# Zero products ahead of the first matmuls, another order of the first K chunks, a bf16 exp, and FFN norms two steps later, in four interleaved layers

## The chip, the core and the metric

The kernel runs on one NeuronCore of a Trainium2 chip. A core has a matrix engine (TensorE, "PE" in the profile; its weight loads are shown as "PEld"), three engines for elementwise work (VectorE, "DVE"; ScalarE, "ACT"; GpSimd, "POOL"), and SyncE ("SP"), whose queue here issues all the transfers. Each engine works through its own list of instructions in order and waits on semaphores for what others make. Data lie in SBUF (128 partitions), products in PSUM (eight banks of 128 x 512 fp32). The metric is the device time of one execution in microseconds; 0.2% of it is about 3 us.

## The reference

Four layers over x of shape (1, 2048, 1024) in bf16: A, B, A, B, each with a residual and a normalization ahead of it. A is linear attention with 32 heads of width 32, B is a gated feed-forward block (FFN) with F = 3584.

```python
def A(x, wqkv, wo):
    q, k, v = split(x @ wqkv)                       # 32 heads of 32
    phi = lambda t: where(t > 0, t + 1, exp(t)) + 1e-6
    pq, pk = phi(q), phi(k)
    kv = einsum("bhsd,bhse->bhde", pk, v)
    z = einsum("bhsd->bhd", pk)
    num = einsum("bhqd,bhde->bhqe", pq, kv)
    den = einsum("bhqd,bhd->bhq", pq, z)[..., None] + 1e-6
    return (num / den).merge_heads() @ wo

def B(x, w_gate, w_up, w_down):
    return ((x @ w_gate) * (x @ w_up)) @ w_down

x = A_x
for _ in range(2):
    x = x + A(layernorm(x), A_wqkv, A_wo)
    x = x + B(layernorm(x), B_w_gate, B_w_up, B_w_down)
```

## The kernel before

X stays in SBUF for the whole program, as 16 tiles of 128 tokens; four tiles make a group of 512 tokens. The order of all work is written out by hand: what the program records first on an engine runs first there. Buffers come from three free lists, in the order in which they were put back: 16 slots of 128 x 4096 bf16, 13 temporaries of 128 x 512 fp32, eight PSUM banks.

**Start (L99 to L143, L918 to L925).** SP issues the loads of X tiles 0 and 1, the first 512 columns of K's weights (a "slab" of 1 MB, L96), X tiles 2 and 3, the second K slab, X 4, the first V slab, and so on. Then, for tiles 0 to 3, the normalization is recorded: `ln_stats` (DVE: two `bn_stats` L158, one aggregation L159), `ln_norm` (ACT: the reciprocal deviation as a Ln L166 and an Exp L168; DVE: L170 writes the normalized tile `xn`). Only tile 0 is also transposed there. `tr_tile` transposes a normalized tile: for the first group of the first layer by eight PE products with the identity (L187) and one ACT copy (L188), in all other places by a transposing DMA on SP's queue (L182).

**Layer A (`layer_A`, L359).** First 64 chunks of eight matmuls (`kv_chunk`, L369): for each group of 512 tokens the eight K chunks (four tiles, two slabs), then the eight V chunks. A K chunk goes through `phi`: ACT takes the exp of the bank into a temporary (L193), DVE takes min with 1 and adds 1e-6 in place (L194), and adds max(x, 0) from the bank (L195). A V chunk is copied by ACT (L377). At given chunk numbers a plan calls other work: statistics, norms and transposes of the tiles of the next group, the product of K features and V (`kp`, L386), and, in the first layer, scans of the FFN weights for their norms (ACT squares L202, DVE statistics L207). In the first layer the transposes of tiles 1, 2 and 3 stand behind chunks 0, 1 and 3, so PE's order is: transposes of tile 0, chunk of tile 0 with slab 0, transposes of tile 1, chunk of tile 0 with slab 1, transposes of tile 2, chunk of tile 1 with slab 0, and so on.

Then comes a loop over steps i = 0 to 43 (L528). Step i takes the denominators of feature block i - 4 (`den_step`: PE L501, ACT L503 and L506, DVE L509), the Q product of block i (`q_step`: eight matmuls L487, then `phi`), and the output product i - 12 (`out_step`: eight matmuls L517, DVE adds to X at L519). An output product of a group needs all eight feature blocks of that group, so the one of step 20 waits for the L509 of step 19. In the first layer, rows of the down weights are scanned in between (ACT L220, DVE L222). At the end of each step what `ahead_of` (L894) has planned for the FFN is called: for tile u = 0 to 7 its statistics at step 18 + 2u, its norm one step later and its transpose DMA two steps later; weight loads, casts (ACT L312) and sums (DVE L327); and sums over the transposed X (`t_sums`, DVE L349 to L357) at steps 36 to 39. In the first layer the loads and GpSimd casts of raw down weights (L566, L571) start at steps 36 and 40.

**Layer B (`layer_B`)** computes the FFN with seven block products instead of eight, on PE at L646 (gate and up) and L868 (down); its lines are not touched.

Of the kernel before, what the change touches and what calls it, by code (L numbers as in the profile page):

```python
# [9 lines left out]
ACT = mybir.ActivationFunctionType  # L10
ALU = mybir.AluOpType
AX = mybir.AxisListType
BF16 = mybir.dt.bfloat16
F16 = mybir.dt.float16
F32 = mybir.dt.float32
# [19 lines left out]
def kernel(  # L35
# [11 lines left out]
    nc = tc.nc  # L47
    P = 128
# [3 lines left out]
    KD = D // P  # L52
    KH = KD // 2
    KF = F // P
    G = 512
    NG = S // G
    TPG = G // P
    NB = 512
    DC = D // NB
# [7 lines left out]
    small = ctx.enter_context(tc.tile_pool(name="small", bufs=4))  # L67
# [6 lines left out]
    wqkv_v = A_wqkv.rearrange("(k p) n -> p k n", p=P)  # L74
# [7 lines left out]
    temps = Free([const.tile([P, NB], F32, tag=f"f{i}", name=f"f{i}") for i in range(13)])  # L82
    banks = Free([psum.tile([P, NB], F32, tag=f"b{i}", name=f"b{i}") for i in range(8)])

    def v3(s, n):
        return s[:].rearrange("p (k n) -> p k n", n=n)
# [4 lines left out]
    def load_x(t):  # L91
        nc.sync.dma_start(out=X[:, t, :], in_=x_view[:, t, :])

    def load_cols(view, n):
        s = slots.get()
        nc.sync.dma_start(out=v3(s, NB), in_=view[:, :, n * NB:(n + 1) * NB])  # L96
        return s

    nc.scalar.preload_act_table_set("natural_log_exp_and_others")  # L99
    wA = {}  # L100
    load_x(0)
    load_x(1)
    wA["k"] = [load_cols(wqkv_v, DC)]
    load_x(2)
    load_x(3)
    wA["k"].append(load_cols(wqkv_v, DC + 1))
    load_x(4)
    wA["v"] = [load_cols(wqkv_v, 2 * DC)]
    load_x(5)
    load_x(6)  # L110
    wA["v"].append(load_cols(wqkv_v, 2 * DC + 1))
    for t in range(7, NT):
        load_x(t)

    ident = const.tile([P, P], BF16, tag="ident", name="ident")
    make_identity(nc, ident[:])
    mask = const.tile([P, P], F32, tag="mask", name="mask")
# [30 lines left out]
    NST = D // FMAX  # L148
# [2 lines left out]
    xqs = {}  # L151
    lns = {}

    def ln_stats(li, t):
        mv = small.tile([P, 2], F32, tag="mv", name="mv")
        st = small.tile([P, NST, 6], F32, tag="st", name="st")
        for c in range(NST):
            nc.vector.bn_stats(out=st[:, c, :], in_=X[:, t, c * FMAX:(c + 1) * FMAX])  # L158
        nc.vector.bn_aggr(out=mv[:], in_=st[:])  # L159
        lns[(li, t)] = mv  # L160

    def ln_norm(li, t):
        mv = lns[(li, t)]
        half = li % 2 == 1
        rstd = small.tile([P, 1], F32, tag="rstd", name="rstd")
        nc.scalar.activation(out=rstd[:], in_=mv[:, 1:2], func=ACT.Ln, bias=(eps5x if half else eps5)[:],  # L166
                             scale=1.0 / (XS * XS) if half else 1.0)
        nc.scalar.activation(out=rstd[:], in_=rstd[:], func=ACT.Exp, scale=-0.5)  # L168
        xn = xnp.tile([P, D], F16 if half else BF16, tag="xn", name="xn")
        nc.vector.tensor_scalar(out=xn[:], in0=X[:, t, :], scalar1=mv[:, 0:1], scalar2=rstd[:],  # L170
                                op0=ALU.subtract, op1=ALU.mult)
        lns[(li, t)] = xn

    def tr_tile(li, t):
        xn = lns.pop((li, t))
        g, tl = divmod(t, TPG)
        if (li, g) not in xnTs:
            xnTs[(li, g)] = slots.get()
        s = xnTs[(li, g)]
        xnT = (h3 if li % 2 == 1 else v3)(s, NB)  # L180
        if (li, g) != (0, 0):
            nc.sync.dma_start_transpose(out=xnT[:, :, tl * P:(tl + 1) * P], in_=xn[:])  # L182
            return
        b = banks.get()
        pt = b[:].bitcast(BF16).rearrange("p (k n) -> p k n", n=P)
        for k in range(KD):
            nc.tensor.transpose(out=pt[:, k, :], in_=xn[:, k * P:(k + 1) * P], identity=ident[:])  # L187
        nc.scalar.copy(out=xnT[:, :, tl * P:(tl + 1) * P], in_=pt)  # L188
        banks.put(b)

    def phi(b, dst):
        m = temps.get()
        nc.scalar.activation(out=m[:], in_=b[:], func=ACT.Exp)  # L193
        nc.vector.tensor_scalar(out=m[:], in0=m[:], scalar1=1.0, scalar2=1e-6, op0=ALU.min, op1=ALU.add)  # L194
        nc.vector.scalar_tensor_tensor(out=dst, in0=b[:], scalar=0.0, in1=m[:], op0=ALU.max, op1=ALU.add)  # L195
        temps.put(m)

    def scan(i):
# [160 lines left out]
    def layer_A(li, ahead):  # L359
# [3 lines left out]
        def kv_chunk(t, n):  # L363
            g, tl = divmod(t, TPG)
            xnT = v3(xnTs[(li, g)], NB)
            w = v3(wA["k"][n] if n < DC else wA["v"][n - DC], NB)
            b = banks.get()
            for k in range(KD):
                nc.tensor.matmul(out=b[:], lhsT=xnT[:, k, tl * P:(tl + 1) * P], rhs=w[:, k, :],  # L369
                                 start=(k == 0), stop=(k == KD - 1))  # L370
            if n < DC:
                if g not in pks:
                    pks[g] = slots.get()
                phi(b, v3(pks[g], D)[:, tl, n * NB:(n + 1) * NB])
            else:
                c0 = (n - DC) * (NB // P)
                nc.scalar.copy(out=vbs[t % NV][:, c0:c0 + NB // P, 0:P],  # L377
                               in_=b[:].rearrange("p (c f) -> p c f", f=P))
            banks.put(b)
# [15 lines left out]
        def at(step, f, *args):  # L395
            plan.setdefault(step, []).append((f, args))

        NCH = 2 * DC * TPG
        for t in range(TPG, NT):
            i = (t // TPG - 1) * NCH + 3 * (t % TPG)  # L400
            at(i + 3, ln_stats, li, t)
            at(i + 5, ln_norm, li, t)
            at(i + 6, tr_tile, li, t)
        for t in range(NT - TPG):
            at((t // TPG + 1) * NCH + 3, kp, t)
        if li == 0:
            for t, i in ((1, 0), (2, 1), (3, 3)):
                at(i, tr_tile, li, t)
        at(2 * NCH + 4, lambda: wA.update(q=[load_cols(wqkv_v, n) for n in range(DC)]))
        at(3 * NCH + 4, lambda: wA.update(o=[load_cols(wo_v, n) for n in range(DC)]))  # L410
        if li == 0:
# [12 lines left out]
            for i, t0, t1 in ((10, 16, 24), (0, 16, 25), (1, 16, 28), (2, 20, 31), (3, 32, 36), (11, 32, 39),  # L424
# [3 lines left out]
                at(t1, spend, i, 0)  # L428
                at(t1 + 1, spend, i, 1)
        for i in range(NG * NCH):  # L430
            q, j = divmod(i, NCH)
            half, j = divmod(j, DC * TPG)
            tl, n = divmod(j, DC)
            kv_chunk(q * TPG + tl, half * DC + n)
            for f, args in plan.get(i, []):
                f(*args)
        slots.put(*wA.pop("k"), *wA.pop("v"))
# [43 lines left out]
        def q_step(g, c):  # L481
            xnT = v3(xnTs[(li, g)], NB)
            w = v3(wA["q"][c // (NB // P)], NB)
            j = c % (NB // P)
            b = banks.get()
            for k in range(KD):
                nc.tensor.matmul(out=b[:], lhsT=w[:, k, j * P:(j + 1) * P], rhs=xnT[:, k, :],  # L487
                                 start=(k == 0), stop=(k == KD - 1))
            pq[(g, c)] = temps.get()
            phi(b, pq[(g, c)][:].bitcast(BF16)[:, 0:G])  # L490
            banks.put(b)
            if c == KD - 1:
                slots.put(xnTs.pop((li, g)))
                if g == NG - 1:
                    slots.put(*wA.pop("q"))
# [279 lines left out]
    def down_seven(q, li, p, hs, wd, load_piece, cast_piece, ORDER, at, run, finish, xrow, nl, W2, load_a, final):  # L775
# [31 lines left out]
        if nl[0] < 4:  # L807
            for u in range(2 * TPG if p == 0 else TPG):
                t = nl[1] * 2 * TPG + u
                at(2 + 7 * u, ln_stats, nl[0], t)  # L810
                at(4 + 7 * u, ln_norm, nl[0], t)
                at(5 + 7 * u, tr_tile, nl[0], t)
# [81 lines left out]
    def ahead_of(li, W):  # L894
        plan = {}

        def at(step, *what):
            plan.setdefault(step, []).append(what)

        for u in range(2 * TPG):  # L900
            at(18 + 2 * u, ln_stats, li, u)
            at(19 + 2 * u, ln_norm, li, u)
            at(20 + 2 * u, tr_tile, li, u)
        at(22, W.load, 0)
        at(28, W.load, 1)
        for i in range(4):
            at(25 + i, W.cast, 0, i)
            at(34 + i, W.cast, 1, i)
            at(36 + i, t_sums, li, 0, i)
        at(35, W.sums, 0)  # L910
        at(41, W.sums, 1)
        if li == 1:
            at(36, prep_load, 0)
            at(38, prep_load, 1)
            at(40, prep_cast, 0)
        return plan

    for t in range(TPG):  # L918
        ln_stats(0, t)
        ln_norm(0, t)  # L920
        if t == 0:
            tr_tile(0, 0)
    for li in (0, 2):
        W = Weights(li)
        layer_A(li, ahead_of(li + 1, W))  # L925
        layer_B(li + 1, W)
# [30 lines left out]
```

## Time and profile before

| | |
|---|---|
| Median of three runs | 1515.85 us (1515.51 to 1516.08) |
| The profiled execution, its own time | 1515.59 us |
| its span, first to last instruction | 1513.8 us |
| PE busy | 1499.7 us (99%), 7155 matmuls |
| DVE busy | 952.5 us (63%) |
| ACT busy | 736.2 us (49%) |
| POOL busy | 90.0 us (6%) |
| DMA engines, mean share | 51.6% on SP's queue, 164 GB/s |

The profile is one execution. The span leaves out what lies before the first and behind the last instruction, so it is 1.79 us shorter than the execution's own time. "Busy" counts overlapping matmuls once; a PE that is 99% busy can still run at a lower clock. A line such as `L369 PE MATMUL b<-s,s` names the line of the kernel, the engine, the operation, and the buffers written and read (`b` a bank, `s` a slot, `f` a temporary). Where an instruction's engine was idle before it, the idle time and what ended it stand in brackets.

The program's stretches, by PE's lines in the chain that ended last: opening until 20.5 us, K and V of the first layer until 130 us, its Q and output steps until 255.8 us, the first FFN until 763.5 us, then the second pair of layers.

### The profile page before, as it was taken

To read this page: it belongs to the slowest core of one execution; us is meant where nothing else is said; L and a number is where in the kernel's file an instruction comes from. 1 tells how busy PE (TensorE), PEld (TensorE's weight loads), DVE (VectorE), ACT (ScalarE), POOL (GpSimd) and SP (SyncE) were. 2 spreads that over 40 slices of the span, in tenths; PEclk is the share of its full clock that TensorE was granted. 3 is DMA by queue.
4 is the path that set the end of the run, shared out by engine and by line. 5 is a ranking of instruction groups with operands and counts; after the bars stand their busy time and mean duration, and the time that the engine had idled before them with its cause. 6 is when DMAs were issued, how large, how long until landed. Compare 5 with 4: busy or idle time off the path is not lost.

```text
span 1513.8 us, 18314 instructions
## 1 busy us (share of the span) xinstructions
PE 1499.7 (99%) x7155; PEld 689.1 (46%) x7155; DVE 952.5 (63%) x1595; ACT 736.2 (49%) x1111; POOL 90.0 (6%) x46
## 2 busy tenths in 40 slices
PE   7999999999999999999999999999999999999999
PEld 3454444444444444444445444444444444444444
DVE  6567998988677566667355467854444853444452
ACT  4677875777535477762133365523334222333420
POOL 0000004963000000000000000000000000000000
PEclk9999999999999999999999999999999999999999
DMA  7696246475358788758413300563333678333523
GB/s 239 152 302 225 84 90 189 121 218 159 117 135 240 239 264 263 243 197 247 160 28 84 84 1 8 148 234 139 140 111 129 165 258 342 113 139 139 193 75 129
DMA packets 213399, 247.61 MB, mean 164 GB/s; under 512 B 68416, under 2 KB 189248, under 8 KB 202560
## 3 DMA queue, kind: packets, MB, share of 16 engines
q1 hardware_dynamic: 213312, 246.44, 51.6%
q8 instruction: 56, 0.92, 0.2%
q14 instruction: 31, 0.25, 0.0%
HBM read 189.79 MB, written 40.89 MB: 152 GB/s over the span
## 4 chain that ended last, share of the span: by engine, by line
PE 94%; DVE 4%; ACT 1%; DMA 1%; issue 0%; SPq 0%
PE b L646 45%; PE b L868 22%; PE b L369 12%; PE b L517 6%; PE b L487 6%; PE b L386 1%; DVE dmx L222 1%; PE b L501 1%; ACT s L202 1%; DVE wst L207 1%; DVE f L195 1%; DMA s<-in_A_wqkv_dram 1%; DVE f L194 1%; ACT f L193 0%; DVE s L195 0%; PE b L469 0%
## 5 line engine op out<-in xcount | busy, mean ns | idle before, releaser
L646 PE MATMUL b<-s,s 128*128 128x512 f16 x3136 | 677.5, 379 | 0.0
L646 PEld LDWEIGHTS <-s 128*128 128x128 f16 x3136 | 306.9, 98 | 370.0
L868 PE MATMUL b<-s,s 128*128 128x512 f16 x1568 | 339.1, 379 | 0.0
L662 DVE TENSOR_TENSOR f<-f,b 128x512 f32<-128x512 f32 x232 | 159.0, 686 | 229.1 <-ACT f L651 214.6
L651 ACT COPY f<-b 128x512 f32<-128x512 f32 x284 | 165.9, 584 | 228.0 <-PE b L646 228.0
L868 PEld LDWEIGHTS <-s 128*128 128x128 f16 x1568 | 153.4, 98 | 185.0
L369 PE MATMUL b<-s,s 128*128 128x512 bf16 x1024 | 225.0, 381 | 2.5 <-DMA s<-in_A_wqkv_dram 2.2
L369 PEld LDWEIGHTS <-s 128*128 128x128 bf16 x1024 | 100.3, 98 | 122.7 <-issue 3.9
L193 ACT ACTIVATE f<-b 128x512 f32<-128x512 f32 x128 | 75.5, 595 | 106.5 <-PE b L369 85.7
L613 ACT ACTIVATE s<-s,scw 128x1792 f16<-128x1792 bf16 x48 | 83.1, 1785 | 90.7 <-DMA s<-in_B_w_down_dram 52.7
L312 ACT ACTIVATE s<-s,scw 128x1024 f16<-128x1024 bf16 x112 | 122.9, 1152 | 3.3 <-DMA s<-in_B_w_gate_dram 2.1
L657 ACT COPY b<-b 128x512 f32<-128x512 f32 x104 | 59.2, 570 | 128.3 <-PE b L646 128.3
L517 PE MATMUL b<-s,s 128*128 128x512 bf16 x512 | 118.5, 379 | 1.9 <-DVE s L509 1.9
L487 PE MATMUL b<-s,s 128*128 128x512 bf16 x512 | 120.3, 379 | 0.0
L571 POOL TENSOR_SCALAR s<-s,scw 128x1024 f16<-128x1024 bf16 x28 | 88.3, 3170 | 263.4 <-DVE X L519 246.1
L194 DVE TENSOR_SCALAR f<-f 128x512 f32<-128x512 f32 x128 | 53.9, 421 | 75.2 <-ACT f L193 74.3
L665 DVE SCALAR_TENSOR_TENSOR s<-f,b 128x512 f16<-128x512 f32 x108 | 74.1, 686 | 40.9 <-PE b L646 24.5
L665 DVE SCALAR_TENSOR_TENSOR s<-f,f 128x512 f16<-128x512 f32 x116 | 82.5, 711 | 4.0
L158 DVE BATCH_NORM_STATS2 st<-X 128x6 f32<-128x512 bf16 x128 | 81.8, 680 | 4.4 <-DMA X<-in_A_x_dram 4.4
L517 PEld LDWEIGHTS <-s 128*128 128x128 bf16 x512 | 50.1, 98 | 62.6 <-DVE s L509 2.4
L487 PEld LDWEIGHTS <-s 128*128 128x128 bf16 x512 | 50.0, 98 | 59.6
L841 DVE SCALAR_TENSOR_TENSOR X<-b,kap,f 128x512 bf16<-128x512 f32 x48 | 32.7, 744 | 60.6 <-PE b L868 60.6
(80 smaller groups left out, 850.6 us busy)
## 6 DMA issues: line engine op xcount, KB each, us to landing
s<-wc SPq DMA_DIRECT2D x56, 1024.0 KB, 6.2
s<-dc SPq DMA_DIRECT2D x32, 896.0 KB, 6.3
wc<-s SPq DMA_DIRECT2D x28, 1024.0 KB, 4.9
s<-in_B_w_down_dram SPq DMA_DIRECT2D x24, 896.0 KB, 5.1
s<-in_B_w_down_dram SPq DMA_DIRECT2D x14, 1024.0 KB, 7.4
s<-in_B_w_gate_dram SPq DMA_DIRECT2D x28, 512.0 KB, 5.8
s<-in_B_w_up_dram SPq DMA_DIRECT2D x28, 512.0 KB, 6.8
s<-in_A_wqkv_dram SPq DMA_DIRECT2D x12, 1024.0 KB, 8.9
```

Of the source, the lines that this page charges most:

```text
L158: nc.vector.bn_stats(out=st[:, c, :], in_=X[:, t, c * FMAX:(c + 1) * FMAX])
L312: nc.scalar.activation(out=h, in_=v, func=ACT.Copy, scale=scw[:, m:m + 1])
L369: nc.tensor.matmul(out=b[:], lhsT=xnT[:, k, tl * P:(tl + 1) * P], rhs=w[:, k, :], start=(k == 0), stop=(k == KD - 1))
L487: nc.tensor.matmul(out=b[:], lhsT=w[:, k, j * P:(j + 1) * P], rhs=xnT[:, k, :], start=(k == 0), stop=(k == KD - 1))
L517: nc.tensor.matmul(out=b[:], lhsT=v3(pqs[g], G)[:, c, tl * P:(tl + 1) * P], rhs=v3(M[n], NB)[:, c, :], start=(c == 0), stop=(c == KD - 1))
L571: nc.gpsimd.tensor_scalar(out=h3(s, D)[:, i, :], in0=v3(s, D)[:, i, :], scalar1=scw[:, 2:3], scalar2=None, op0=ALU.mult)
L613: nc.scalar.activation(out=v.bitcast(F16)[:, r * w:(r + 1) * w], in_=v[:, r * w:(r + 1) * w], func=ACT.Copy, scale=scw[:, 2:3])
L646: nc.tensor.matmul(out=o[m][:], lhsT=W.get(j, m, st[i - 1], k), rhs=mv[i - 1][:, k, :], start=start and k == 0, stop=stop and k == KH - 1, ...
L651: nc.scalar.copy(out=d[m][:], in_=o[m][:])
L662: nc.vector.tensor_tensor(out=d[m][:], in0=d[m][:], in1=o[m][:], op=ALU.add)
L665: nc.vector.scalar_tensor_tensor(out=hv[:, 2 * (j % 2) + r, g * G:(g + 1) * G], in0=x[:], scalar=HS, in1=y[:], op0=ALU.mult, op1=ALU.mult)
L868: nc.tensor.matmul(out=bank[(key, tl)][:], lhsT=lhs(i, j, tl), rhs=h3(wd[2 * pi + j // WPC], NB)[:, j % WPC, :], start=(j == 0 and i in (1 ...
```

## The change

Four edits go together.

- **Zero products.** A temporary is set to zero, and PE multiplies it with itself into an unused bank: 11 products of 128 x 512 recorded ahead of everything else on PE, four more behind the transposes of tile 0. Their results are not read.
- **Opening.** The first K slab is loaded in two DMAs of four 128-row blocks each. Tile 1's first half statistics are recorded ahead of tile 0's norm. The ACT copy behind PE transposes is split into two halves (L188 becomes two copies). The first eight chunks are taken by slab: tiles 0 to 3 with slab 0, then tiles 0 to 3 with slab 1; before, both slabs of one tile followed each other. The transposes of tiles 1, 2 and 3 stand behind chunks 0, 1 and 2. X tiles 2 and 3 are issued between the first and the second slab, as before.
- **exp in bf16.** `phi` keeps its temporary as bf16: ACT writes the exp in bf16, DVE's min and add run on bf16, and the last operation reads bf16.
- **FFN norm.** In `ahead_of`, statistics, norm and transpose of each tile come two steps later, `t_sums` three steps later.

```diff
-    def load_cols(view, n):
+    def load_cols(view, n, parts=1):
         s = slots.get()
-        nc.sync.dma_start(out=v3(s, NB), in_=view[:, :, n * NB:(n + 1) * NB])
+        w = KD // parts
+        for r in range(parts):
+            nc.sync.dma_start(out=v3(s, NB)[:, r * w:(r + 1) * w, :],
+                              in_=view[:, r * w:(r + 1) * w, n * NB:(n + 1) * NB])
         return s
...
-    wA["k"] = [load_cols(wqkv_v, DC)]
+    wA["k"] = [load_cols(wqkv_v, DC, 2)]
...
+    warm = temps.get()
+    nc.vector.memset(warm[:], 0.0)
+    warmb = banks.get()
+
+    def warm_up(n):
+        for _ in range(n):
+            nc.tensor.matmul(out=warmb[:], lhsT=warm[:].bitcast(BF16)[:, 0:P], rhs=warm[:].bitcast(BF16)[:, 0:NB],
+                             start=True, stop=True)
+
+    warm_up(11)
...
-    def ln_stats(li, t):
-        mv = small.tile([P, 2], F32, tag="mv", name="mv")
-        st = small.tile([P, NST, 6], F32, tag="st", name="st")
-        for c in range(NST):
+    def ln_stats(li, t, parts=tuple(range(NST))):
+        if parts[0] == 0:
+            lns[(li, t)] = small.tile([P, NST, 6], F32, tag="st", name="st")
+        st = lns[(li, t)]
+        for c in parts:
             nc.vector.bn_stats(out=st[:, c, :], in_=X[:, t, c * FMAX:(c + 1) * FMAX])
-        nc.vector.bn_aggr(out=mv[:], in_=st[:])
-        lns[(li, t)] = mv
+        if parts[-1] == NST - 1:
+            mv = lns[(li, t)] = small.tile([P, 2], F32, tag="mv", name="mv")
+            nc.vector.bn_aggr(out=mv[:], in_=st[:])
...
-        nc.scalar.copy(out=xnT[:, :, tl * P:(tl + 1) * P], in_=pt)
+        nc.scalar.copy(out=xnT[:, 0:KH, tl * P:(tl + 1) * P], in_=pt[:, 0:KH])
+        nc.scalar.copy(out=xnT[:, KH:KD, tl * P:(tl + 1) * P], in_=pt[:, KH:KD])
...
         m = temps.get()
-        nc.scalar.activation(out=m[:], in_=b[:], func=ACT.Exp)
-        nc.vector.tensor_scalar(out=m[:], in0=m[:], scalar1=1.0, scalar2=1e-6, op0=ALU.min, op1=ALU.add)
-        nc.vector.scalar_tensor_tensor(out=dst, in0=b[:], scalar=0.0, in1=m[:], op0=ALU.max, op1=ALU.add)
+        e = m[:].bitcast(BF16)[:, 0:NB]
+        nc.scalar.activation(out=e, in_=b[:], func=ACT.Exp)
+        nc.vector.tensor_scalar(out=e, in0=e, scalar1=1.0, scalar2=1e-6, op0=ALU.min, op1=ALU.add)
+        nc.vector.scalar_tensor_tensor(out=dst, in0=b[:], scalar=0.0, in1=e, op0=ALU.max, op1=ALU.add)
...
+        order = [(g * TPG + tl, h * DC + n) for g in range(NG) for h in range(2) for tl in range(TPG)
+                 for n in range(DC)]
...
-            for t, i in ((1, 0), (2, 1), (3, 3)):
-                at(i, tr_tile, li, t)
+            for t in range(1, TPG):
+                at(t - 1, tr_tile, li, t)
+            order[0:8] = [(t, n) for n in range(DC) for t in range(TPG)]
...
-            kv_chunk(q * TPG + tl, half * DC + n)
+            kv_chunk(*order[i])
...
-            at(18 + 2 * u, ln_stats, li, u)
-            at(19 + 2 * u, ln_norm, li, u)
-            at(20 + 2 * u, tr_tile, li, u)
+            at(20 + 2 * u, ln_stats, li, u)
+            at(21 + 2 * u, ln_norm, li, u)
+            at(22 + 2 * u, tr_tile, li, u)
...
-            at(36 + i, t_sums, li, 0, i)
+            at(39 + i, t_sums, li, 0, i)
...
-    for t in range(TPG):
+    ln_stats(0, 0)
+    ln_stats(0, 1, (0,))
+    ln_norm(0, 0)
+    tr_tile(0, 0)
+    ln_stats(0, 1, (1,))
+    ln_norm(0, 1)
+    for t in range(2, TPG):
         ln_stats(0, t)
         ln_norm(0, t)
-        if t == 0:
-            tr_tile(0, 0)
+    warm_up(4)
+    temps.put(warm)
+    banks.put(warmb)
```

More of the change, by code (lines that the diff above doesn't have):

```diff
@@ L430, in layer_A @@
         for i in range(NG * NCH):
-            q, j = divmod(i, NCH)
-            half, j = divmod(j, DC * TPG)
-            tl, n = divmod(j, DC)
-            kv_chunk(q * TPG + tl, half * DC + n)
+            kv_chunk(*order[i])
             for f, args in plan.get(i, []):
```

## The prediction

> **What bounds the kernel now.** Page first: TensorE (PE) is busy 1499.7 us of a 1513.8 us span, and 94% of the chain that ended last is PE work. From 20.52 us on, matmuls of 512 columns follow each other every 0.216 us (128 of them take 27.63 us in the chain). So time can only be won where PE waits or runs slower. The waits of PE are four:
>
> ```profile
> PE b L187 <- DVE xn L170: 6.4, 1, 6.4
> PE b L369 <- DMA s<-in_A_wqkv_dram: 2.2, 1, 2.2
> PE b L517 <- DVE s L509: 1.9, 1, 1.9
> PE b L369 <- DVE s L195: 0.2, 1, 0.2
> ```
>
> Columns: us in total, times, longest. The first two lie in the opening, the third at 191.49 to 193.42 us, the fourth at 119.6. Next the opening itself, in order of time (start, duration):
>
> ```profile
> 9.62 3.57 PE L369 MATMUL b<-s,s 128*128 128x512 bf16 x8 [2.22 <-DMA s<-in_A_wqkv_dram]
> ...
> 10.33 1.29 DVE L158 BATCH_NORM_STATS2 st<-X 128x6 f32<-128x512 bf16 x2 [0.88 <-DMA X<-in_A_x_dram]
> ...
> 14.04 2.29 PE L369 MATMUL b<-s,s 128*128 128x512 bf16 x8
> ...
> 14.48 0.29 ACT L166 ACTIVATE rstd<-mv,eps 128x1 f32<-128x1 f32 x1 [2.05 <-DVE mv L159]
> 14.80 0.20 ACT L168 ACTIVATE rstd<-rstd 128x1 f32<-128x1 f32 x1
> ...
> 14.91 0.58 ACT L193 ACTIVATE f<-b 128x512 f32<-128x512 f32 x1
> ...
> 15.39 1.00 ACT L188 COPY s<-b 128x1024 bf16<-128x1024 bf16 x1
> ...
> 16.62 3.62 PE L369 MATMUL b<-s,s 128*128 128x512 bf16 x16
> ...
> 20.52 27.79 PE L369 MATMUL b<-s,s 128*128 128x512 bf16 x128
> ```
>
> The reader is to see three things. PE starts slow: the first chunk's 8 matmuls are 0.427 us apart (9.62 to 12.99 us, 3.37 us), a later chunk takes 1.73. ACT works strictly in program order: the exp of the first chunk, done by PE at 13.2, and the copy L188 of tile 1's transposes, done at 14.04, both stand until ACT has made the rstd of tile 3 (14.80 to 15.00), because all four norms are written ahead of the layer. And PE had something to do in that time: chunk (0,1), tile 0 against the second K slab, at 14.04. I write (t,n) for tile and slab.
>
> Then the end of the trace, for the clock after PE falls idle (us, busy times, then granted clock, DMA):
>
> ```profile
> 1510.00:1513.30 3.30, 0.47 (x3) 0.00 (x0) 0.75 (x1) 0.00 (x0) 0.00 (x0) 1.00 0.12 40
> 1513.40:1513.80 0.40, 0.00 (x0) 0.00 (x0) 0.00 (x0) 0.00 (x0) 0.00 (x0) 0.50 0.00 0
> ```
>
> The last matmul ends at 1510.46; by 1513.4 the grant is 0.50. Some 2.9 us of idleness were enough. Last, VectorE (DVE) at the third wait:
>
> ```profile
> 190.96 0.68 DVE L519 TENSOR_TENSOR X<-X,b 128x512 bf16<-128x512 bf16 x1
> 191.55 1.28 DVE L158 BATCH_NORM_STATS2 st<-X 128x6 f32<-128x512 bf16 x2
> 192.86 0.21 DVE L159 BATCH_NORM_AGGREGATE mv<-st 128x2 f32<-128x12 f32 x1
> 192.99 0.37 DVE L509 TENSOR_TENSOR s<-f,f 128x512 bf16<-128x512 bf16 x1
> ```
>
> DVE has no idle time from 161 us to there, and the statistics of FFN tile 0 (step 18) stand just ahead of the L509 that PE needs.
>
> **Opening.** The zero products need one memset on DVE, which is idle until 3.56, and 11 cold matmuls, 11 x 0.427 = 4.7 us, on a PE idle until 6.36: cost nothing; started later than 1.6 us, they would push the transposes one for one. The four further ones (0.9 to 1.7 us) stand before chunk (0,0) but inside its wait for the slab, which ends at 9.57. The half statistics of tile 1 (0.68) fill DVE's 0.66 us gap while ACT makes the first rstd; X tile 1 lands near 4.1 (issue 1.18, 2.9 to landing). The split slab adds one SP issue (0.43) ahead of X tile 2; both land behind the same bytes, so I price it at nothing, and at up to 0.43, one for one, if the issue time shows.
>
> With the slab in halves and the clock up by 8 us, chunk (0,0) runs its first half near 8 and its second at 9.6 to 10.5; transposes of tile 1 until 10.95. Before, these were done at 13.85. But the next PE instruction is now chunk (1,0), not (0,1). It needs the copy of tile 1, and that stands on ACT behind the rstd of tile 3. That chain is not shortened: X tile 2 starts its statistics at 10.33, behind the whole first slab, and ACT is free at 15.0. Exp at 14.91, first half copy at 15.39; a 512-column ACT pass from PSUM takes 0.59 (row L377, 0.59), 0.05 to PE (L188 ends 8.44, weight load 8.49): chunk (1,0) starts at **16.03**. PE sits idle from 10.95, 5.1 us. Queued behind it on PE: everything.
>
> From there before and after compare simply. Before, chunk (1,0) started at 16.62 with (0,0), (0,1) and two tiles' transposes done, and 20.52 was reached with four chunks and all transposes. After, at 16.03 one chunk and one transposed tile are done; to come are three chunks and two tiles. Each tile's transposes are followed by exp, copy, chunk: last matmul to its end 0.16, exp starts 0.05 later, ACT's next instruction 0.49 after that, half copy 0.59, PE 0.05: 1.34 between chunks, against 0.45 for transposes alone. Warm: 3 x 1.73 + 2 x 1.34 = 7.87, end 23.9, **3.4 us later** than 20.52. The halved copy does what it can here: whole, it would add 0.42 (1.01 against 0.59) for each tile.
>
> The clock: by the end-of-trace row, 2.9 us idle lower it, and here 5.1 us pass. Chunk (1,0) then costs 3.37 for 1.73, the next transposes 0.85 for 0.45, mostly under the exp: 1.4 to 2.5 more, by whether the full grant returns with the first 3 us of work or as late as in the opening, where it took 9.62 to 14.85. I take 1.9. Opening: **+5.3** (3.4 if the clock stays; 5.9 at the late end).
>
> The Trainium skill, "TensorE: Matmul & The Clock Gate", Part 1, speaks against this order: it wants no idle gap above some 3.4 us, since the activity window is free-running and a whole idle window lowers the clock. By that rule a 5.1 us gap holds a whole window only half the time, and the opening would be an even draw between +3.4 and +5.3; the row, with its 2.9 us, makes the drop the rule.
>
> **exp in bf16.** ACT's exp keeps its 0.59. L194 (0.42 on f32) becomes bf16 in and out, which no row shows with this size. Bounds: 0.42, unchanged, and half of L170, a bf16 pass of 1024 columns in 0.543, 0.27; no reason for a loss. I take 0.30, nearest to L170 in type: 0.12 saved. L195 stays at 0.69: it reads PSUM, and L665 has 0.69 with PSUM and 0.71 from SBUF. Of 128 such pairs only those ahead of a late PE count: 5 before 119.8 (0.6 against a wait of 0.23) and 7 from 161 to 193 (0.84). In the second layer PE never waits, so nothing.
>
> The skill's "VectorE: DVE Perf Modes", in its perf-mode tier table, puts tensor_scalar on bf16 in SBUF at 693 ns against 1227 in fp32 for 2048 elements; scaled to L194 that is an estimate of 0.24, or 1.3 us instead of 0.84 in the second window, and the sum is the same either way.
>
> **FFN norm two steps later.** Statistics, rstd, norm and transpose DMA of eight tiles go from steps 18 to 34 to steps 20 to 36, the X sums from 36-39 to 39-42. Ahead of the L509 of step 19 goes 1.44 us (191.55 to 192.99): of the 1.93 us wait 0.49 would stay, and bf16 takes that. Steps 18 and 19 leave DVE 2 x (3.67 - 2.0) us to recover, so no later L509 is late. What is late next: X sums three steps of 1.73 later, the first from 246.5 to near 252, needed at 257.4; the last near 260 (behind weight sums), needed at 263.4. On SP the raw-weight loads stand behind the last transpose DMA, up to 3.5 us later than 242.5; POOL's casts began at 248.6, take 4 x 3.17, and DVE first used them at 273. Cost nothing; without these margins of 3 to 5 us, one for one. Gain: **-1.93 - 0.23 = -2.16**; at least 1.4 if bf16 saves nothing.
>
> **Sum.** Own time 1515.59 (span 1513.80 and 1.79 around it) + 5.3 - 2.16 = 1518.7; the median 1515.85 lies 0.26 higher: **1519.0**.
>
> **Rivals.** (a) The clock stays up through the gap: +3.4 - 2.16, 1517.1. For it: only one row shows a drop. (b) DVE's waits do not go, since something in the later norms takes their place: +5.3 - 0.2, 1520.9. For it: DVE is 96% busy from 150 to 200 us; against: 1.44 us leave the very queue. (c) The other side: X tile 2 lands early. Its landing at 10.3 sets chunk (1,0) at a fixed distance of 5.7. If the halved slab lets it land at 7.5, PE resumes at 13.2, the gap is 2.3 us and the clock holds: end at 21.1, +0.6 - 2.16, 1514.3. It is faster than before once X tile 2 lands more than 1.3 us sooner; against it, the same bytes go first. Even with no wait for tile 1 the 1.34 between chunks remains: 10.47 + 3 x 3.07 = 19.7, and -0.8 - 2.2 = -3.0 is the floor. (d) Zero products don't raise the clock: chunk (0,0) then ends near 12.5, still ahead of 16.03; no other time than the forecast's.
>
> **How the numbers follow.** Forecast with (d) 0.62, (a) 0.18, (b) 0.10, (c) 0.06, other 0.04. What a measurement can tell is about 0.2%, 3.0 us. The forecast's own range, opening 4.8 to 5.9, ends at +2.6 to +3.7, and about three quarters of it lie beyond 3.0: 0.46, with (b) and rests 0.59 slower. Within: 0.16 + 0.18 and a third of (c), 0.36. Faster by that: what is left of (c) and a little of the rest, 0.05, since the floor only touches it. The range takes in (a) and (b): 1516.8 to 1521.2.
>
> **What would show it.** ACT's exp (0,0) after tile 3's rstd near 14.9; PE idle from about 11 to 16 with wait on ACT's copy; 8 matmuls 0.427 apart after it; L194 near 0.3; no PE wait at 120 and 193; FFN's first matmul about 3 us later than 255.64. PE resuming before 14, or X tile 2's statistics before 9, makes it wrong.

## The result, and the profile after

Over 14 runs each the changed kernel takes 1519.0 us (1517.83 to 1521.78) against 1515.76 (1514.74 to 1516.4): ratio 1.0024, 95% interval 1.0015 to 1.0032. It is slower, by an amount just above what can be told from no change, and its runs lie four microseconds apart where those of before lie within 1.7. The profiled execution is one of the fastest: 1518.05 us, span 1516.0.

The view of who waited for whom, engine PE, for the changed kernel (us in total, times, longest):

```profile
PE b L386 <- ACT s L203: 6.3, 3, 4.9
PE b L124 <- DVE f L119: 1.4, 1, 1.4
PE b L202 <- DVE xn L185: 0.7, 1, 0.7
PE b L534 <- DVE s L526: 0.3, 1, 0.3
```

L386 is the chunk's matmul (L369 before), L203 the first half of the copy behind the transposes, L526 the product that was L509. The waits of 2.2 and 1.9 us of before are gone, and so is the one of 0.2; in their place stands ACT's copy, once for 4.9 us and twice for 0.7. The timeline of the opening (start, duration, idle time before and what ended it):

```profile
1.44 4.21 PE L124 MATMUL b<-f 128*128 128x512 bf16 x11 [1.44 <-DVE f L119]
...
7.63 2.16 PE L386 MATMUL b<-s,s 128*128 128x512 bf16 x8
...
9.43 1.29 DVE L172 BATCH_NORM_STATS2 st<-X 128x6 f32<-128x512 bf16 x2 [0.38 <-DMA X<-in_A_x_dram]
9.63 0.61 PE L202 MATMUL b<-ident,xn 128*128 128x128 bf16 x8
...
13.91 0.20 ACT L183 ACTIVATE rstd<-rstd 128x1 f32<-128x1 f32 x1
14.02 0.58 ACT L210 ACTIVATE f<-b 128x512 bf16<-128x512 f32 x1
...
14.49 0.58 ACT L203 COPY s<-b 128x512 bf16<-128x512 bf16 x1
...
15.13 3.54 PE L386 MATMUL b<-s,s 128*128 128x512 bf16 x8 [4.88 <-ACT s L203]
...
19.83 1.90 PE L386 MATMUL b<-s,s 128*128 128x512 bf16 x8 [0.72 <-ACT s L203]
...
22.90 5.35 PE L386 MATMUL b<-s,s 128*128 128x512 bf16 x24 [0.72 <-ACT s L203]
```

Chunk (0,0) is done near 9.6 us, its exp stands until tile 3's reciprocal deviation (rstd) is ready (13.91 to 14.11), the copy of tile 1 stands behind that exp, and PE idles from 10.24 to 15.13. Its next eight matmuls take 3.4 us instead of 1.73. The same stretches with PE's busy time, granted clock, DMA share and GB/s:

```profile
8.30:11.60 3.30, 1.83 (x14) 1.00 1.09 374
11.70:15.00 3.30, 0.00 (x0) 1.00 1.09 356
15.10:18.40 3.30, 3.27 (x8) 0.50 1.08 364
18.50:24.00 5.50, 4.06 (x31) 1.00 1.07 374
```

The granted clock (the grant, below) is still full in the idle stretch and falls to half just as PE resumes (15.07); one fully busy stretch later it is back (18.48). The step that before began at 20.52, behind four chunks and all transposes, begins at 22.90 + 1.73 = 24.63: +4.1 us. The first FFN starts at 257.74 instead of 255.64: +2.1. So some 2 us come back in between, and nothing after that: the span grows by 2.2.

The four microseconds of scatter go with the clock. Each run has its mean granted clock on record: the six slowest, from 1519.87 us up, have 0.997; of the eight others four have 0.999, three 0.998 and one 0.997. Half clock for 3.41 us, as in the profile, takes 0.001 off the mean; for 10.24 us it takes 0.003. The runs of the kernel before that were taken beside the experiments all have 1.000.

The third place is a late product, at 245.4 us. First PE, then DVE:

```profile
245.43 4.92 PE L534 MATMUL b<-s,s 128*128 128x512 bf16 x22 [0.30 <-DVE s L526]
```

```profile
242.17 0.54 DVE L185 TENSOR_SCALAR xn<-X,mv,rstd 128x1024 f16<-128x1024 bf16 x1
242.62 0.42 DVE L526 TENSOR_TENSOR s<-f,f 128x512 bf16<-128x512 bf16 x1
242.96 0.68 DVE L536 TENSOR_TENSOR X<-X,b 128x512 bf16<-128x512 bf16 x1
243.56 1.28 DVE L172 BATCH_NORM_STATS2 st<-X 128x6 f32<-128x512 bf16 x2
244.87 0.21 DVE L175 BATCH_NORM_AGGREGATE mv<-st 128x2 f32<-128x12 f32 x1
245.00 0.37 DVE L526 TENSOR_TENSOR s<-f,f 128x512 bf16<-128x512 bf16 x1
```

The statistics of FFN tile 7, moved to step 34, now stand ahead of the last group's last L526 (step 35), for which the output product of step 36 waits.

### The profile page after: what moved, and what is told of

Same layout as the page of the kernel before. It is cut to its first block, busy times and chain, and to the rows that moved or that the text cites. A ratio compares the mean times of both kernels' runs of the same rounds, so it can differ in the third digit from the quotient of the medians.

```text
span 1516.0 us, 18351 instructions
## 1 busy us (share of the span) xinstructions
PE 1503.7 (99%) x7170; PEld 689.9 (46%) x7170; DVE 940.2 (62%) x1596; ACT 737.4 (49%) x1115; POOL 89.5 (6%) x46
## 4 chain that ended last, share of the span: by engine, by line
PE 98%; DVE 1%; DMA 0%; ACT 0%; issue 0%; SPq 0%; DVEq 0%
PE b L663 45%; PE b L885 22%; PE b L386 15%; PE b L504 7%; PE b L534 7%; PE b L403 1%; PE b L518 1%; PE b L486 0%; DMA X<-in_A_x_dram 0%; DVE st L172 0%; DVE X L536 0%; ACT s L203 0%; DVE s L526 0%; DVE xn L185 0%; ACT f L210 0%
## 5 line engine op out<-in xcount | busy, mean ns | idle before, releaser
L386 PE MATMUL b<-s,s 128*128 128x512 bf16 x1024 | 224.6, 381 | 6.4 <-ACT s L203 6.3
L386 PEld LDWEIGHTS <-s 128*128 128x128 bf16 x1024 | 100.0, 98 | 126.8 <-ACT s L203 7.1
L210 ACT ACTIVATE f<-b 128x512 bf16<-128x512 f32 x128 | 75.6, 596 | 112.1 <-PE b L386 90.9
L211 DVE TENSOR_SCALAR f<-f 128x512 bf16<-128x512 bf16 x128 | 37.0, 289 | 86.7 <-ACT f L210 86.1
```

## The experiments

Theory: the opening loses, because ACT's order holds chunk (1,0) and the clock falls meanwhile; the bf16 exp and the later norms win part of it back. The first pair takes the change apart.

**The opening alone.** The changed kernel with `phi`, the norm steps and `t_sums` of before:

```diff
-        e = m[:].bitcast(BF16)[:, 0:NB]
-        nc.scalar.activation(out=e, in_=b[:], func=ACT.Exp)
+        nc.scalar.activation(out=m[:], in_=b[:], func=ACT.Exp)
...
-            at(20 + 2 * u, ln_stats, li, u)
+            at(18 + 2 * u, ln_stats, li, u)
...
-            at(39 + i, t_sums, li, 0, i)
+            at(36 + i, t_sums, li, 0, i)
```

> The kernel before with the zero products and the whole opening of the change, exp in f32 and the FFN norms at their old steps. Theory (the opening loses, the other two edits win back): opening 4.1 us as in the profile of after, up to 8 where the clock comes back a window later, so 1520.9 us in the middle (1519.8 to 1524), and both DVE waits of before (0.2 and 1.9) back in the profile. Rival (the opening is neutral or better and bf16 or the norms cost the time): 1516 or less.

Measured: 1520.49 us (1520.04 to 1522.59, 5 runs) against 1515.38; ratio 1.0035, 1.0022 to 1.0047. Its profile, of the run of 1522.59 (mean granted clock 0.996; the other four have 0.998), has DVE's two waits of before, 0.25 and 1.94 us, at 126.3 and 199.9, and shows how the late end of the scatter arises. Windows of PE, as above:

```profile
10.80:14.10 3.30, 0.00 (x0) 1.00 1.09 358
14.20:17.50 3.30, 2.42 (x6) 0.50 1.08 364
17.60:20.90 3.30, 2.62 (x13) 0.50 1.09 362
21.10:24.40 3.30, 3.30 (x15) 0.50 1.05 387
24.50:28.00 3.50, 2.82 (x15) 1.00 0.36 127
```

Here the half clock lasts from 14.18 to 24.42 us. Two stretches in which PE was busy 2.42 and 2.62 of 3.3 us did not bring the full grant back; one that was full did. The four chunks end at 27.0 instead of 24.6.

**The other two edits alone**, in the kernel before:

```diff
-        nc.scalar.activation(out=m[:], in_=b[:], func=ACT.Exp)
+        e = m[:].bitcast(BF16)[:, 0:NB]
+        nc.scalar.activation(out=e, in_=b[:], func=ACT.Exp)
...
-            at(18 + 2 * u, ln_stats, li, u)
+            at(20 + 2 * u, ln_stats, li, u)
...
-            at(36 + i, t_sums, li, 0, i)
+            at(39 + i, t_sums, li, 0, i)
```

> The kernel before with only the bf16 exp and the FFN norms two steps later. Theory: the waits of 1.93 and 0.23 go, the new one of 0.30 stays: 1515.76 - 1.86 = 1513.9 us. Rival (these two edits are what costs): 1518 or more. A third reading, that the waits only move with the late opening: 1515.7.

Measured: 1513.63 us (1512.44 to 1514.23, 11 runs) against 1515.38; ratio 0.9988, 0.9979 to 0.9996. +5.1 and -1.75 add to +3.4; the whole change has +3.2. Within the noise (the first interval is almost 4 us wide) the two add.

Then each of the two by itself, in the kernel before. **bf16 exp only** (the first hunk above):

> The kernel before with the bf16 exp alone. Theory (each min-and-add is 0.13 us shorter, seven of them stand between DVE's last idle time and the late product): the wait of 0.23 goes, the one of 1.93 shrinks by 0.9 to about 1.0: 1.15 us less than before. Rival (the late wait comes from the norm's statistics alone, so bf16 gives nothing): as before within 0.3; or (bf16 is enough alone): 2.1 less.

Measured: 1513.85 us (1513.20 to 1515.02) against 1515.27; ratio 0.9991, 0.9982 to 1.0000, at the edge of what can be told. PE's waits in its profile:

```profile
PE b L187 <- DVE xn L170: 6.3, 1, 6.3
PE b L370 <- DMA s<-in_A_wqkv_dram: 1.4, 1, 1.4
PE b L518 <- DVE s L510: 1.1, 1, 1.1
```

The wait of 0.2 is gone, the one of 1.93 is 1.14. (The first wait for a slab is 0.8 shorter too, with the loads unchanged: the slab landed at 8.72 us in this run, at 9.57 in the profile before. A comparison of two single profiles carries that much scatter.)

**Later norms only** (the other two hunks):

> The kernel before with the FFN norms two steps later alone. Theory: 1.44 us of statistics and aggregation leave the queue ahead of the late product, so the wait of 1.93 shrinks to about 0.5, the 0.23 stays, and the new wait at step 36 is 0.3 to 0.6: 0.9 to 1.1 us less than before. Rival (two steps later only moves the wait to step 36): as before within 0.3.

Measured: 1514.56 us (1514.10 to 1515.18) against 1515.27; ratio 0.9996, 0.9987 to 1.0005, which is not told from no change; the waits are what counts here:

```profile
PE b L517 <- DVE s L509: 0.9, 2, 0.5
PE b L369 <- DVE s L195: 0.2, 1, 0.2
```

The two are 0.54 at 192.1 and 0.35 at 242.5: the wait shrinks by 1.4 and a new one stands 50 us later. Neither edit is enough alone for the wait at 193; together they clear it.

**What in the opening costs: the clock.** 21 more zero products behind tile 1's transposes fill most of the gap; the temporary and its bank are given back after chunk 8 instead of ahead of the layer:

```diff
             for t in range(1, TPG):
                 at(t - 1, tr_tile, li, t)
+            at(0, warm_up, 21)
+            at(8, lambda: (temps.put(warm), banks.put(warmb)))
...
     warm_up(4)
-    temps.put(warm)
-    banks.put(warmb)
```

> The changed kernel with 21 more zero products (21 x 0.216 = 4.5 us) right behind tile 1's transposes, inside the 4.9 us in which PE waits for ACT's copy; nothing else moves. Theory (part of the loss, and all of the scatter of 1517.8 to 1521.8, is the clock that falls in the gap): chunk (1,0) still starts near 15.1 us but takes 1.73 instead of 3.4; 1.6 us less than the fastest mode of the change, 1516.4 us, with runs within 0.8 us of each other. Rival (the scatter and the cost have another cause, the gap itself alone): 1518 to 1519 with the same scatter.

Measured: 1516.17 us (1515.68 to 1516.51, 11 runs); ratio to before 1.0004, 0.9995 to 1.0012. The scatter of four microseconds has become one of 0.8, all runs have a mean granted clock of 1.000, and the median is 2.8 lower than the change's, or 2.5 when each is taken against its own runs of before (+0.8 and +3.2). In its profile chunk (1,0) still starts only behind the copy, at 14.64, but takes 1.73 us:

```profile
14.64 1.90 PE L386 MATMUL b<-s,s 128*128 128x512 bf16 x8
...
17.71 1.90 PE L386 MATMUL b<-s,s 128*128 128x512 bf16 x8 [0.72 <-ACT s L203]
```

**What in the opening costs: ACT's order.** The changed kernel, with the norms of tiles 2 and 3 recorded behind the copies:

```diff
-    for t in range(2, TPG):
-        ln_stats(0, t)
-        ln_norm(0, t)
+    ln_stats(0, 2)
...
-            for t in range(1, TPG):
-                at(t - 1, tr_tile, li, t)
+            at(0, tr_tile, li, 1)
+            at(0, ln_norm, li, 2)
+            at(0, ln_stats, li, 3)
+            at(1, tr_tile, li, 2)
+            at(1, ln_norm, li, 3)
+            at(2, tr_tile, li, 3)
```

> The changed kernel, but the norms of tiles 2 and 3 recorded behind tile 1's and tile 2's copies instead of ahead of the layer, so that ACT's copy of tile 1 does not stand behind the rstd of tile 3. Theory (ACT's program order holds PE): chunk (1,0) starts near 10.9 instead of 15.1, the four slab-0 chunks are done near 18.7 instead of 24.6: 5.9 us less than the profiled run of the change, 1512.2 us (1511.5 to 1513). Rival (PE waits for X tiles 2 and 3 or their transfers anyway): no better than 1517.

Measured: 1512.15 us (1511.69 to 1513.08, 11 runs); ratio to before 0.9979, 0.9970 to 0.9988. It beats both kernels, by 3.2 us and, each against its own runs of before, by 6.5. Timeline of ACT in its opening:

```profile
9.97 0.60 ACT L210 ACTIVATE f<-b 128x512 bf16<-128x512 f32 x1 [1.11 <-PE b L386]
10.46 0.58 ACT L203 COPY s<-b 128x512 bf16<-128x512 bf16 x1
10.93 0.60 ACT L204 COPY s<-b 128x512 bf16<-128x512 bf16 x1
11.41 0.32 ACT L181 ACTIVATE rstd<-mv,eps 128x1 f32<-128x1 f32 x1
```

The exp follows its chunk at once, the copy follows the exp, and the deviation of tile 2 comes after. Chunk (1,0) starts at 11.10; X tiles 2 and 3 land as in the change (9.39 and 10.09), so chunk (1,0) did not need them; in the change they held it only by way of ACT's order. Three waits of 0.72 for the copy remain. For an order that also fills those with chunks of another tile there is no measurement. Set beside the kernel with the other two edits alone (-1.75 us), this one (-3.2) shows what the new opening is worth once ACT's order fits it: 1.5 us.

**The order by slab.** The changed kernel with the chunks and transposes in the order of before, norms still ahead of the layer:

```diff
-            for t in range(1, TPG):
-                at(t - 1, tr_tile, li, t)
-            order[0:8] = [(t, n) for n in range(DC) for t in range(TPG)]
+            for t, i in ((1, 0), (2, 1), (3, 3)):
+                at(i, tr_tile, li, t)
```

> The changed kernel with the chunk order and the transposes of before: tile 0 with both slabs first, norms of tiles 2 and 3 still ahead of the layer. Theory (the order by slab is what takes away PE's work during the wait for ACT): chunk (0,1) runs at the landing of the second slab, near 13.1 us, and chunk (1,0) follows near 15.3 without a wait; four chunks done near 19.2 if the clock holds through the gap of 3 us: 1512.4 us, up to 1514.5 where it falls. Rival (the order doesn't matter, the loss lies in other parts of the opening): 1518 to 1519.

Measured: 1513.93 us (1512.47 to 1514.90); ratio 0.9991, 0.9982 to 1.0000. In the profile, which is its fastest run, PE waits 2.90 us for the second slab, to 13.25, the clock holds, and the four chunks are done at 19.32. So the new order is what took away the work under ACT's chain. The rest of the opening is not shown to gain anything: 19.32 is 1.2 us sooner than 20.52, but the unchanged opening reached the same point at 19.43 in the profile with bf16 alone, and in the median this kernel (-1.2 us) is no faster than the other two edits alone (-1.75). The 2.9 us gap costs the clock in most of its runs: the four fastest, up to 1513.20, have a mean granted clock of 1.000, the seven from 1513.47 up 0.999, which takes 1.5 us or more at half clock; the longest half clock at a program's end, in the profile of ACT's order mended, is 1.3 us.

**The zero products.** The changed kernel without the 15 products and their memset:

```diff
-    nc.vector.memset(warm[:], 0.0)
...
-    warm_up(11)
...
-    warm_up(4)
```

> The changed kernel without the 15 zero products and their memset. Theory (ACT's order sets when chunk (1,0) starts, so what the zero products speed up ends well before it): chunk (0,0) runs cold and ends near 11.5 us instead of 9.7, chunk (1,0) still starts near 15.1, mostly cold as before; 1518 to 1521 us, as the change. Rival 1 (the zero products are what the change loses by): 1516 or less. Rival 2 (they are worth what they speed up, here 2 us and more): above 1521.

Measured: 1518.28 us (1517.19 to 1520.16, 11 runs); ratio to before 1.0022, 1.0013 to 1.0030. Within the scatter this is the change's own time: the zero products bring nothing there. Its profile, of the run of 1520.16, has chunk (0,0) cold from 8.12 to 11.5 us, and chunk (1,0) still starts where ACT lets it:

```profile
15.25 3.59 PE L384 MATMUL b<-s,s 128*128 128x512 bf16 x8 [2.67 <-ACT s L201]
```

The same three lines taken out of the kernel with ACT's order mended:

> The run with ACT's order mended (norms of tiles 2 and 3 behind the copies), without the zero products and their memset. Theory (the zero products were worthless in the change only since PE stood idle behind them): chunk (0,0) ends near 11.5 us instead of 9.8, chunk (1,0) starts near 13.2 instead of 11.1, and the slab-0 chunks run cold until a window without waits: 2 to 5 us more than the 1512.15 with them, 1514.2 to 1517. Rival (the zero products are worth nothing, or cost, in any order): within 0.5 us of 1512.15.

Measured: 1513.82 us (1513.52 to 1516.03, 11 runs) against 1512.15 with them: 1.7 us, and less than the two or more that were expected. That is all of the 1.5 us that the opening gains with ACT's order mended: without them this kernel (-1.45 us) is no faster than the other two edits alone (-1.75). So the zero products pay only where nothing later holds PE. Its profile is one of two runs near 1516:

```profile
7.93 3.60 PE L384 MATMUL b<-s,s 128*128 128x512 bf16 x8 [0.68 <-ACT s L201]
...
13.06 3.60 PE L384 MATMUL b<-s,s 128*128 128x512 bf16 x8 [0.68 <-ACT s L201]
...
17.98 1.90 PE L384 MATMUL b<-s,s 128*128 128x512 bf16 x8 [0.68 <-ACT s L201]
```

Two cold chunks, then the full grant (16.95). The nine runs near 1513.7 may have it 3.41 us sooner, after one cold chunk; no profile of them shows it.

## Why the prediction was right

The median was met, and the mechanism holds at every larger step: PE idles behind ACT's order, the clock falls, the two DVE waits go. That it was met to 0.1 us is luck: X tile 2 landed 0.9 sooner than reckoned, the clock cost some 0.6 more, and a new wait of 0.30 came up, which cancel.

- **PE resumes 5.7 us behind X tile 2.** 15.13 - 9.41 = 5.72. Right. The landing itself was put at 10.3 and came at 9.4: an issue more ahead of it was priced at nothing to +0.43, and 0.9 was gained. That is one term mis-sized. It is not this run alone: X tile 2 lands at 8.7 to 9.5 us in the seven profiles with the split slab, at 9.4 to 10.7 in the four without.
- **1.34 us between chunks.** Chunks start at 19.83 and 22.90: 3.07 apart, the 1.73 + 1.34 of the prediction.
- **The clock falls in the gap.** Shown by the profile (half from 15.07), and by the filled gap, in which the wait stays and 2.5 us go. All 14 runs, at 0.997 to 0.999, had the drop, so the even draw that the prediction sets beside its row did not hold here. The price was 1.9, from 1.4 to 2.5. In the profiled run it is 1.6 (3.4 against 1.73, and the rest hidden), but the median pays about 2.5, and the profile of the opening alone shows far more, since the clock does not come back in "the first 3 us of work" or the next 3 if waits for ACT lie in them. This is the step that failed in size, and it made the upper end, 5.9 for the opening, too low: that profile has 6.5 (27.0 against 20.52).
- **Opening +5.3.** Measured +5.1 by the opening alone, in the median; +4.1 in the profile of the change. By the medians, each against its own runs of before, the clock is 2.5 of it (+3.2 less +0.8), ACT's order 4.0 (+0.8 less -3.2), and 1.5 go off for what the new opening gains with that order mended: 5.0 in sum.
- **bf16: 0.30 for L194, 0.84 us off the wait.** The row is 289 ns (the 0.24 that the prediction sets beside it was too low), and the wait shrinks by 0.79 in the kernel with bf16 alone. Right.
- **Norms: 1.44 off the wait, and "no later L509 is late".** The first is right (1.39). The second failed: by 0.30 in the change, 0.35 alone. The prediction reckoned with steps 18 and 19; the small operations of the down-weight norm around step 33 (L283 to L296, 1.5 us) and tile 7's statistics fill DVE ahead of step 35.
- **Sum of the waits -2.16**: measured -2.16 + 0.30 = -1.86 in the waits and -1.75 in time.
- **Rivals.** (a), the clock staying up, is the kernel with the filled gap, 1516.2 where 1517.1 was said. (b) is excluded by the waits: the new one is 0.30, not 2. (c) happened by a third: X tile 2 came 0.9 sooner, short of the 1.3 at which it would have decided. (d) is void: the zero products do raise the clock, at 4.83 in the change's profile; it didn't help.
- **Chances.** The forecast's +2.6 to +3.7 lies beyond 3.0 by two thirds if spread evenly, not three quarters; nothing hangs on it.

## What to carry to other kernels

Where an engine takes its work in program order, a reordering on one engine has to be followed into the lists of the others: here the matmuls were ready, and two operations of 0.3 and 0.2 us for a tile two places later, recorded early, held them for 4.0 us (chunk (1,0) at 15.13, and at 11.10 with ACT's order mended). Before a start is made faster, look at what the next wait ends on: speeding up work in front of a fixed wait only lengthens the wait, and a long one costs the clock as well. And a time that scatters over several microseconds where the kernel before did not is itself a sign; look at the mean granted clock of every run before comparing medians.

## What the runs showed of the hardware

- The grant changes in steps of 3.41 us (half clock for 3.41 us in the change, for 10.24 in the opening alone). It fell after a stretch with no PE work at all (11.7 to 15.0 us), and at the end of two programs after stretches with some: 0.47 of 3.3 us in the kernel before, 1.21 of 3.41 with ACT's order mended:

```profile
1505.69:1509.10 3.41, 1.21 (x6) 1.00 0.19 63
1509.11:1510.30 1.19, 0.00 (x0) 0.50 0.00 0
```

- It held through two stretches with a little more work in the run with the old chunk order:

```profile
8.60:12.00 3.40, 1.47 (x12) 1.00 1.09 358
12.00:15.40 3.40, 2.15 (x16) 1.00 1.09 355
```

- To come back it wanted nearly a full stretch: 3.27 of 3.3 us was enough, 2.62 was not. So 43% of work in a stretch kept the full clock, while 79% did not restore it; where between 35 and 43%, and between 79 and 99%, the limits lie is not measured. By these figures a gap of 4.9 us always costs the clock (an estimate: however it falls on the steps of 3.41, one of them has at least 2.4 us without work, and so at most 1.0 with), and one of 2.9 us only where it falls badly.
- Transposes on PE seem to count as work for it: in the kernel before the grant came at 14.90, at the end of a stretch (from 11.49) with 2.3 us of chunk matmuls and 1.06 us of transposes, while in the opening alone 2.42 us of matmuls and no transposes did not do.
- Products on zeros raised it like others, 3.4 us after the first one (1.44 to 4.83) in the change, later in the four other profiles with them (5.17, 5.57, 7.24, 7.35).
- The granted clock in these views starts at 1.00 and says nothing until its first change: in the stretch from 13.06 us of the last run above, ahead of the grant at 16.95, eight matmuls take 3.4 us, which is half clock, and that run's mean is 1.000.
- The first slab in two halves landed whole at 8.0 to 8.9 us in seven profiles, in one piece at 8.7 to 10.0 in four. Why is open.
